# Larger rest bursts, paired score banks and a new order inside an attention slot

## The chip, the cores and the metric

The kernel runs on one core of a Trainium2 chip. TensorE (PE) multiplies, PEld is its weight load, VectorE (DVE) and ScalarE (ACT) read the product banks (PSUM, eight banks of 512 fp32 values in each of 128 partitions), GpSimd (POOL) and SyncE (SP) start DMAs. The metric is the device time of one execution in microseconds; less is better.

## The reference, cut to what matters

```python
xn = layernorm(A_x)                                   # 2048 tokens x 576
q  = (xn @ wq) -> 32 heads of 128                     # wq is 576 x 4096
k, v = last 512 rows of the caches, 16 heads, each used by 2 query heads
p  = softmax(q k^T / sqrt(128));  o = p v
s  = o.reshape(2048, 4096) @ wo                       # wo is 4096 x 576
g  = silu(B(xn))                                      # layernorm, gelu, shifts, w1, w2, w3, w4
out = A_x + s * g
```

The 576 input columns are four full chunks of 128 rows and a rest of 64 rows. The change concerns the attention, `s`.

## The kernel before, in words

The 2048 tokens are four blocks of 512. One attention "slot" `u` (0 to 127) is one query head of one block, `u = block * 32 + head`. In a slot the kernel issues the four score products of head `u` (`stage_s`, a 128x512 bank each: 128 keys by 512 tokens), the query product of head `u+1` (`stage_q`), and the value products of head `u-1` (`stage_v`, two halves of eight 128x129 matmuls; the 129th column of `v_sb` is one, so that it gives the softmax's denominator). ACT takes the exponential of each score bank into `pT`. DVE copies the finished query product to `qT` (bf16), inverts the denominators and scales the value products into `o`. SP transposes `o` by DMA into `oT`, and in the slots from `WO0 = 45` and from 65 and 97 PE also multiplies an earlier block's `oT` by `wo`, in five groups, one in a slot: four of 32 matmuls with 512 columns (L269, copied out by ACT at L279) and a fifth, of 128 matmuls with 64 columns, for the last 64 output columns (copied out at L291). The product of the last block stands around the last slots and behind them.

The query product of a head is four matmuls with 128 rows of `wq` (L526) and one with the 64 rest rows. The first four heads (`PLAIN`) take the rest as a fifth matmul padded with zeros. For all others the rest is computed for four heads together (`rest_q`, L511): two matmuls with 64 rows each stand side by side on the two halves of PE's rows, for two of the heads straight into their query banks, for the other two into two score banks. ACT copies those two to `rq` (L516, 128x512 each), and DVE adds `rq` while it makes `qT` (L534). The rest weights are loaded with every block of `wq` (`load_wq`, L339 and L346), 30 times in all, on POOL's queue.

PSUM holds three single score banks (`ps_sc`), two query banks (`ps_pq`), two value banks (`ps_po`) and one bank for the `wo` product (`ps_wo`). The finished `o` of 18 heads fit in `o_pool`.

The order of PE, SP and POOL is written out by hand (`manual_schedule`) in a loop over the slots; ACT's and DVE's order is set by a planner when the program is built. Small steps of layernorm for later blocks are put into slots by `fill`, transposes by `turn`, the `wo` products by `pe_fill`. The beginning, before slot 0, is written out for all engines: transposes of the first block on PE into three score banks (L470), copies to `xT_b` on DVE (L478) and ACT (L476), key transposes (L486), and the first two heads' query products (L707).

The stretch behind the attention (the MLP branch B and the end) starts some 466 us into the span. The change touches none of its lines.

Of the kernel before, what the change touches and what calls it, by code (L numbers as in the profile page):

```python
# [8 lines left out]
P = 128  # L9
ACT = mybir.ActivationFunctionType  # L10
ALU = mybir.AluOpType
# [20 lines left out]
def kernel(  # L32
# [266 lines left out]
    with ExitStack() as actx:  # L299
# [10 lines left out]
        wq_b = [res.tile([P, NDC, 4 * Dh], BF16, name=f"wq_b{i}") for i in range(NWQ)]  # L310
# [37 lines left out]

# [16 lines left out]
        def prep_k(g):  # L365
            st = {}
            src = kst_t[g // 4][:, (g % 4) * W:(g % 4 + 1) * W]

            def tr(kc):
                if kc == 0:  # L370
                    st["ps"] = ps_wo.tile([P, W], BF16, name="ps_k", tag="wo")
                nc.tensor.transpose(out=st["ps"][:, kc * P:(kc + 1) * P], in_=src[:, kc * P:(kc + 1) * P],
                                    identity=ident[:, :])
                if kc == KCH - 1:
                    with tc.high_priority(offset=HP):
                        nc.vector.tensor_copy(out=kT[:, g, :], in_=st["ps"][:, :])

            return [lambda kc=kc: tr(kc) for kc in range(KCH)]

# [15 lines left out]
        for w in wq_b:  # L395
            nc.gpsimd.memset(w[DR:, NF, :], 0.0)
        with tc.manual_schedule(engines={SP}):
            load_k(0, nc.sync, 2)
            for m0 in (0, 2 * Dh):
                cols = slice(m0, m0 + 2 * Dh)  # L400
                nc.sync.dma_start(out=wq_b[0][:, 0:NF, cols],
# [998 lines left out]
```

## Time and profile before

| what | us |
|---|---|
| median of three runs | 817.04 (816.65 to 817.09) |
| the profiled execution's own time | 817.54 |
| its span, first to last instruction | 815.9 |
| PE busy | 804.7 |
| ACT busy | 445.4 |
| DVE busy | 445.6 |

The span is what the profile's times are counted in; the execution's own time lies 1.6 us above it. Matmuls overlap, so a matmul's own duration (379 ns for 512 columns) is longer than the distance to the next one in an undisturbed row of them; distances are read from the timeline, where several equal instructions stand as one row with their count, the start of the first and the time to the end of the last.

### The profile page before, as it was taken

Reading aid. Unit: us, or ns where it says so; the run is one execution under the profiler, and the core shown is the slowest. Engines: PE = TensorE matmul, PEld = TensorE weight load, DVE = VectorE, ACT = ScalarE, POOL = GpSimd, SP = SyncE. Lnnn points to the kernel's source line nnn. Section 1 sums busy time; section 2 is a strip of 40 time slices with the busy share of each in tenths; the row PEclk is TensorE's granted clock in tenths of the full one; section 3 lists DMA queues with packets and bytes.
Section 4 is the critical chain, followed back from the end, with each engine's and each line's share of the span. In section 5 each row is a group of like instructions: output and inputs, shape, how many; then the busy total and the mean of one; then the engine's idle time right before and its main releaser. Section 6 shows DMA issues by size and latency. Waiting matters only on the chain. (4 is left out here: it accounts for less than half of the span.)

```text
span 815.9 us, 19891 instructions
## 1 busy us (share of the span) xinstructions
PE 804.7 (99%) x8157; PEld 469.0 (57%) x8239; DVE 445.6 (55%) x1379; ACT 445.4 (55%) x798; POOL 125.2 (15%) x211
## 2 busy tenths in 40 slices
PE   9999999999999999999999999999999999999997
PEld 6655655466545666545666556555555555555555
DVE  6868685128832679642566439353246636655413
ACT  7888887338833788833888542033343333335620
POOL 3333321201101111100210301272000000000000
PEclk9999999999999999999999999999999999999999
DMA  7995998109842756410674461399100410330101
GB/s 210 170 186 153 169 190 144 59 9 165 167 70 59 147 97 136 109 45 14 132 133 81 83 93 59 92 303 229 55 2 16 93 44 16 48 89 16 45 15 39
DMA packets 137710, 81.26 MB, mean 100 GB/s; under 512 B 114288, under 2 KB 127888, under 8 KB 137616
## 3 DMA queue, kind: packets, MB, share of 16 engines
q1 hardware_dynamic: 123536, 39.85, 29.2%
q0 software_dynamic: 12832, 38.85, 18.8%
q8 instruction: 65, 1.06, 0.6%
q10 hardware_dynamic: 1248, 1.25, 0.4%
q14 instruction: 29, 0.24, 0.1%
HBM read 46.89 MB, written 6.93 MB: 66 GB/s over the span
## 5 line engine op out<-in xcount | busy, mean ns | idle before, releaser
L549 ACT ACTIVATE pT<-sc 128x512 bf16<-128x512 f32 x512 | 286.7, 599 | 95.7 <-PE sc L545 80.0
L545 PE MATMUL sc<-qT,kT 128*128 128x512 bf16 x507 | 168.5, 379 | 0.1
L564 PEld LDWEIGHTS <-pT 128*128 128x128 bf16 x2048 | 134.5, 98 | 52.6 <-issue 11.0
L564 PE MATMUL po<-v_sb,pT 128*128 128x129 bf16 x2048 | 158.0, 220 | 0.3
L1033 PE MATMUL ph<-xT_b,w_s 64*128 64x512 bf16 x976 | 127.4, 376 | 0.0
L526 PE MATMUL psq<-xT_b,wq_b 128*128 128x512 bf16 x451 | 121.8, 379 | 3.0
L1070 PE MATMUL pm<-w_s,h 64*128 64x512 bf16 x864 | 122.2, 377 | 0.0
L1051 ACT ACTIVATE h<-ph 128x512 bf16<-128x512 f32 x67 | 39.4, 597 | 132.7 <-PE ph L1033 130.5
L569 DVE TENSOR_TENSOR o<-po,ri_b 128x256 bf16<-128x256 f32 x256 | 107.8, 421 | 6.4
L1070 PEld LDWEIGHTS <-h 64*128 64x128 bf16 x1728 | 71.1, 94 | 54.9
L269 PE MATMUL pswo<-wo_sb,oT 128*128 128x512 bf16 x434 | 101.3, 379 | 0.6
L269 PEld LDWEIGHTS <-oT 128*128 128x128 bf16 x1024 | 64.8, 98 | 54.3
L1070 PE MATMUL pr<-w_s,h 64*128 64x64 bf16 x864 | 90.3, 189 | 0.0
L536 DVE CAST qT<-psq 128x512 bf16<-128x512 f32 x64 | 44.0, 688 | 74.2 <-PE psq L511 42.9
L1033 PEld LDWEIGHTS <-w_s 64*128 64x128 bf16 x1152 | 56.1, 94 | 48.2 <-issue 0.6
L526 PEld LDWEIGHTS <-wq_b 128*128 128x128 bf16 x506 | 49.4, 98 | 59.3 <-issue 0.8
L534 DVE TENSOR_TENSOR qT<-psq,rq 128x512 bf16<-128x512 f32 x62 | 42.8, 691 | 69.7 <-ACT pT L549 59.7
L1049 DVE COPY hx<-ph 128x512 f32<-128x512 f32 x55 | 38.0, 692 | 60.3 <-PE ph L1033 60.3
L339 POOL DMA_DIRECT2D wq_b<-in_A_wq_dram x30 | 23.1, 770 | 264.6 <-PE sc L545 252.7
L568 DVE RECIPROCAL ri_b<-po 128x2 f32<-128x2 f32 x256 | 42.4, 165 | 32.0 <-PE po L564 26.7
L545 PEld LDWEIGHTS <-kT 128*128 128x128 bf16 x512 | 45.7, 98 | 20.7 <-DVE qT L534 0.5
L516 ACT ACTIVATE rq<-sc 128x512 f32<-128x512 f32 x62 | 33.6, 594 | 8.2 <-PE sc L511 8.2
(168 smaller groups left out, 700.2 us busy)
## 6 DMA issues: line engine op xcount, KB each, us to landing
wq_b<-in_A_wq_dram POOLq DMA_DIRECT2D x30, 512.0 KB, 4.7
wo_sb<-in_A_wo_dram POOLq DMA_DIRECT2D x8, 576.0 KB, 7.0
w_s<-in_B_w_dram POOLq DMA_DIRECT2D x9, 512.0 KB, 6.0
w_s<-in_B_w_dram POOLq DMA_DIRECT2D x10, 288.0 KB, 5.0
w_s<-in_B_w_dram POOLq DMA_DIRECT2D x4, 576.0 KB, 5.6
s_b<-s_dram SPq DMA_DIRECT2D x4, 576.0 KB, 7.3
x_b<-in_A_x_dram SPq DMA_DIRECT2D x4, 576.0 KB, 7.6
out_dram<-o SPq DMA_DIRECT2D x15, 144.0 KB, 1.8
```

The source lines that it names most:

```text
L269: nc.tensor.matmul(ps, lhsT=oT_t[qb * Hq + h][:, tt, :], rhs=wo_sb[:, h, lo:hi], start=(i == 0), stop=(i == Hq - 1))
L526: nc.tensor.matmul(psq[:, :], lhsT=w[:, kc, hh * Dh:(hh + 1) * Dh], rhs=xT_b[qb % 2][:, kc, :], start=(kc == 0 and not (two and hh == 1)), ...
L534: behind["qT"] = nc.vector.tensor_tensor(out=qT[:, :], in0=psq[:, :], in1=rq_t.pop(u)[:, :], op=ALU.add)
L536: nc.vector.tensor_copy(out=qT[:, :], in_=psq[:, :])
L545: nc.tensor.matmul(sc[:, :], lhsT=kT[:, g, kc * P:(kc + 1) * P], rhs=qT_t[u][:, :], start=True, stop=True)
L549: behind["exp"] = nc.scalar.activation(out=pT[:, :], in_=sc[:, :], func=ACT.Exp, scale=SCALE)
L564: nc.tensor.matmul(po[:, j, :], lhsT=pTs[kc][:, tt * P:(tt + 1) * P], rhs=v_sb[:, g, kc, 0:Dh + 1], start=(kc == 0), stop=(kc == KCH - 1))
L568: nc.vector.reciprocal(out=ri, in_=po[:, :, Dh])
L569: nc.vector.tensor_tensor(out=o[:, t0:t0 + 2, :], in0=po[:, :, 0:Dh], in1=ri.unsqueeze(2).to_broadcast([P, 2, Dh]), op=ALU.mult)
L1033: nc.tensor.matmul(ps[i][:, :], lhsT=lhsT, rhs=xT[half, kc, :], start=first, stop=last, skip_group_check=True)
L1051: nc.scalar.activation(out=h3[:, :], in_=src[:, :], func=ACT.Gelu_apprx_tanh)
L1070: nc.tensor.matmul(out, lhsT=h3_t[b, fc][half, tt * P:(tt + 1) * P], rhs=w4_s[fc // WS][half, fc % WS, lo:hi], start=key not in started, s ...
```

## The change

- The rest is computed for six heads at a time (16 times) or for four (7 times), by a list of first heads, `BURSTS`. The first two of a burst go into their query banks as before; the next two into the second score pair, the last two of six into the first pair. ACT copies the first of these pairs with one 128x1024 instruction (L528); of the other, DVE copies one half (L525) and ACT the other (L526).
- The rest weights of all heads stay in `wr_sb` (128 x 16 x 128), loaded once by `load_wr`. The plain heads' rest weights lie in `wr_first`, a part of `wo_sb` that is filled later.
- The score banks are two pairs (`sc0`, `sc1`) of two banks each. `stage_s(u, i)` writes a pair with two matmuls, and one 128x1024 exponential reads it (L560).
- The bank for the `wo` product is gone: in the slots with a `wo` group the group's bank is the first half of `sc1`, and both halves of the scores go through `sc0`.
- The order in a slot is: query product, scores of pair 0, fill, values, scores of pair 1, values, with the `wo` matmuls in four parts between. In a slot that issues a burst (`late_q`) the scores of pair 0 come first, and both halves of the values stand ahead of pair 1; if such a slot has a `wo` group too (49, 69 and 101: the fifth groups), that group's first part follows the first scores at once.
- At the beginning the transposes go into one tile of two banks (four chunks) and the other tile (the fifth chunk and two key heads).
- `o_pool` has 12 tiles, and five more lie in `xn_b[3]` until that block is loaded: 17 in place of 18.
- `prep_k` had no caller left and goes.

```diff
--- before.py
+++ after.py
...
         PLAIN = 4
-        wq_b = [res.tile([P, NDC, 4 * Dh], BF16, name=f"wq_b{i}") for i in range(NWQ)]
+        BURSTS = [(4, 6), (10, 6), (16, 6), (22, 6), (28, 4), (32, 6), (38, 6), (44, 6), (50, 4), (54, 4), (58, 6),
+                  (64, 6), (70, 4), (74, 6), (80, 6), (86, 6), (92, 4), (96, 6), (102, 4), (106, 6), (112, 6), (118, 6),
+                  (124, 4)]
+        SPARE = 5
+        spare = xn_b[NB - 1][:].rearrange("p t d -> p (t d)")
+        WO0 = Hq + 13
+        wo_slots = {b * Hq + 1 + i if b > 1 else WO0 + i for b in range(1, NB) for i in range(TB + 1)}
+        x_at = (9, Hq + 14, 2 * Hq + 4)
+        wq_b = [res.tile([P, NF, 4 * Dh], BF16, name=f"wq_b{i}") for i in range(NWQ)]
+        wr_sb = res.tile([P, Hq // 2, Dh], BF16, name="wr_sb")
+        wr_first = wo_sb[:, PLAIN, 0:PLAIN * Dh]
         ri_b = res.tile([P, Hq, TB], FP32, name="ri_b")
...
         qT_pool = pool("qT_pool", 3)
-        pT_pool = pool("pT_pool", 4)
-        pT2_pool = pool("pT2_pool", 3)
-        o_pool = pool("o_pool", 18)
-        ps_sc = pool("ps_sc", 3, PSUM)
+        pT_pool = pool("pT_pool", 5)
+        o_pool = pool("o_pool", 12)
+        ps_sc = pool("ps_sc", 1, PSUM)
         ps_pq = pool("ps_pq", 2, PSUM)
         ps_po = pool("ps_po", 2, PSUM)
-        ps_wo = pool("ps_wo", 1, PSUM)
...
-            eng.dma_start(out=w[:, 0:NF, :],
-                              in_=A_wq[0:NF * P, c0:c0 + 4 * Dh].rearrange("(kc p) m -> p kc m", p=P))
-            if j < PLAIN // 4:
-                eng.dma_start(out=w[0:DR, NF, :], in_=A_wq[NF * P:D, c0:c0 + 4 * Dh])
-                return
-            last = A_wq[NF * P:D, c0:c0 + 4 * Dh].rearrange("p (j two m) -> p j two m", two=2, m=Dh)
+            eng.dma_start(out=w[:, :, :],
+                          in_=A_wq[0:NF * P, c0:c0 + 4 * Dh].rearrange("(kc p) m -> p kc m", p=P))
+            if 1 < j < 8:
+                load_wr(j + 1, 1, eng)
+        def load_wr(j, n, eng):
+            j = j % 8
+            last = A_wq[NF * P:D, :].rearrange("p (j two m) -> p j two m", two=2, m=Dh)
             for k in range(2):
-                eng.dma_start(out=w[k * DR:(k + 1) * DR, NF, 0:2 * Dh].rearrange("p (j m) -> p j m", j=2),
-                              in_=last[:, :, k, :])
+                eng.dma_start(out=wr_sb[k * DR:(k + 1) * DR, 2 * j:2 * (j + n), :],
+                              in_=last[:, 2 * j:2 * (j + n), k, :])
...
             load_wq(1, nc.sync)
+            load_wr(1, 2, nc.sync)
...
         def x_banks():
-            pairs = [ps_sc.tile([P, 2, QB], BF16, name="ps_x", tag="sc") for _ in range(3)]
-            return [pairs[kc // 2][:, kc % 2, :] for kc in range(NDC)]
+            four = [ps_sc.tile([P, 4, QB], BF16, name="ps_x", tag=f"sc{i}") for i in range(2)]
+            return [four[kc // 4][:, kc % 4, :] for kc in range(NDC)], four[1][:, 2:4, :]
...
-        def keys_first(g0, psp, tag):
-            ps = psp.tile([P, 2, W], BF16, name="ps_k2", tag=tag)
+        def keys_first(g0, ps):
...
+        bursts, first_of = {}, {}
+        for u0, n in BURSTS:
+            bursts[u0] = n
+            for i in range(n):
+                first_of[u0 + i] = u0
+        def score_bank(i):
+            return ps_sc.tile([P, 2, QB], FP32, name="sc", tag=f"sc{i}")
+        def wq_main(u, kc):
+            cols = slice(u % 4 * Dh, (u % 4 + 1) * Dh)
+            return wq_b[(u // 4) % NWQ][:, kc, cols] if kc < NF else wr_first[:, cols]
         def rest_q(u, first):
-            w, xT = wq_b[(u // 4) % NWQ], xT_b[u // Hq % 2]
+            xT = xT_b[u // Hq % 2]
             psq_t[u + 1] = ps_pq.tile([P, QB], FP32, name="psq", tag="pq")
-            pss = [first, psq_t[u + 1]] + [ps_sc.tile([P, QB], FP32, name="sc", tag="sc") for _ in range(2)]
+            n = bursts[u]
+            pair = [score_bank(i) for i in ((0,) if u - 1 in wo_slots else (1, 0)[0:n // 2 - 1])]
+            pss = [first, psq_t[u + 1]] + [p[:, i, :] for p in pair for i in range(2)]
             for i, ps in enumerate(pss):
                 half = slice(i % 2 * DR, (i % 2 + 1) * DR)
-                nc.tensor.matmul(ps[:, :], lhsT=w[half, NF, i // 2 * Dh:(i // 2 + 1) * Dh], rhs=xT[half, NF, :],
+                nc.tensor.matmul(ps[:, :], lhsT=wr_sb[half, (u + i) % Hq // 2, :], rhs=xT[half, NF, :],
                                  start=(i > 0), stop=(i != 1), skip_group_check=True)
-            for i in (2, 3):
-                rq_t[u + i] = rq_pool.tile([P, QB], FP32, name="rq")
+            for k, p in enumerate(pair):
+                rq = rq_pool.tile([P, 2, QB], FP32, name="rq")
                 with tc.high_priority(offset=HP):
-                    behind["rq"] = nc.scalar.activation(out=rq_t[u + i][:, :], in_=pss[i][:, :], func=ACT.Copy)
+                    if k:
+                        nc.vector.tensor_copy(out=rq[:, 0, :], in_=p[:, 0, :])
+                        nc.scalar.activation(out=rq[:, 1, :], in_=p[:, 1, :], func=ACT.Copy)
+                    else:
+                        nc.scalar.activation(out=rq[:], in_=p[:], func=ACT.Copy)
+                for i in range(2):
+                    rq_t[u + 2 + 2 * k + i] = rq[:, i, :]
         def stage_q(u):
-            qb, h = divmod(u, Hq)
-            w = wq_b[(u // 4) % NWQ]
-            hh = h % 4
-            two = u >= PLAIN
-            psq = psq_t.pop(u) if two and hh == 1 else ps_pq.tile([P, QB], FP32, name="psq", tag="pq")
-            n = NF if two else NDC
+            qb = u // Hq
+            plain = u < PLAIN
+            pos = 0 if plain else u - first_of[u]
+            psq = psq_t.pop(u) if pos == 1 else ps_pq.tile([P, QB], FP32, name="psq", tag="pq")
+            n = NDC if plain else NF
             for kc in range(n):
-                nc.tensor.matmul(psq[:, :], lhsT=w[:, kc, hh * Dh:(hh + 1) * Dh], rhs=xT_b[qb % 2][:, kc, :],
-                                 start=(kc == 0 and not (two and hh == 1)), stop=(kc == n - 1 and not (two and hh == 0)),
+                nc.tensor.matmul(psq[:, :], lhsT=wq_main(u, kc), rhs=xT_b[qb % 2][:, kc, :],
+                                 start=(kc == 0 and pos != 1), stop=(kc == n - 1 and (plain or pos != 0)),
                                  skip_group_check=True)
-            if two and hh == 0:
+            if not plain and pos == 0:
                 rest_q(u, psq)
...
             with tc.high_priority(offset=HP):
-                if two and hh >= 2:
-                    behind["qT"] = nc.vector.tensor_tensor(out=qT[:, :], in0=psq[:, :], in1=rq_t.pop(u)[:, :], op=ALU.add)
+                if pos >= 2:
+                    behind["qT"] = nc.vector.tensor_tensor(out=qT[:, :], in0=psq[:, :], in1=rq_t.pop(u), op=ALU.add)
                 else:
...
-        def stage_s(u, kc):
+        def stage_s(u, i):
             g = (u % Hq) // REP
-            if kc == 0:
-                pT_t[u] = []
-            first = u == 0 and kc == KCH - 1
-            sc = (ps_po if first else ps_sc).tile([P, QB], FP32, name="sc", tag="po" if first else "sc")
-            nc.tensor.matmul(sc[:, :], lhsT=kT[:, g, kc * P:(kc + 1) * P], rhs=qT_t[u][:, :], start=True, stop=True)
-            if kc == 1:
-                pair_t[u] = pT2_pool.tile([P, 2, QB], BF16, name="pT2")
-            pT = pair_t[u][:, kc - 1, :] if kc in (1, 2) else pT_pool.tile([P, QB], BF16, name="pT")
-            behind["exp"] = nc.scalar.activation(out=pT[:, :], in_=sc[:, :], func=ACT.Exp, scale=SCALE)
-            pT_t[u].append(pT)
-            if kc == KCH - 1:
+            sc = score_bank(0 if u in wo_slots else i)
+            for j in range(2):
+                kc = 2 * i + j
+                nc.tensor.matmul(sc[:, j, :], lhsT=kT[:, g, kc * P:(kc + 1) * P], rhs=qT_t[u][:, :], start=True,
+                                 stop=True)
+            pT = pT_pool.tile([P, 2, QB], BF16, name="pT")
+            nc.scalar.activation(out=pT[:], in_=sc[:], func=ACT.Exp, scale=SCALE)
+            pT_t.setdefault(u, []).extend(pT[:, j, :] for j in range(2))
+            if i == 1:
                 qT_t.pop(u)
...
             if t0 == 0:
-                o_t[u] = o_pool.tile([P, TB, Dh], BF16, name="o")
+                i = u % (12 + SPARE)
+                if i < SPARE and u < x_at[2] - 2 * SPARE:
+                    o_t[u] = spare[:, i * QB:(i + 1) * QB].rearrange("p (a b) -> p a b", a=TB)
+                else:
+                    o_t[u] = o_pool.tile([P, TB, Dh], BF16, name="o")
             o = o_t[u]
...
             oT = oT_pool.tile([P, TB, P], BF16, name="oT")
-            nc.sync.dma_start(out=oT[:], in_=o[:].rearrange("p a b -> p (a b)"), transpose=True)
+            nc.sync.dma_start(out=oT[:], in_=o[:, :, :].rearrange("p a b -> p (a b)"), transpose=True)
             oT_t[u] = oT
...
             def bank(shape, name):
-                return ps_pq.tile(shape, FP32, name=name, tag="pq") if last else ps_wo.tile(shape, FP32, name=name, tag="wo")
+                if last:
+                    return ps_pq.tile(shape, FP32, name=name, tag="pq")
+                half = score_bank(1)[:, 0, :]
+                return half if len(shape) == 2 else half[:, 0:TB * R0].rearrange("p (t r) -> p t r", t=TB)
...
-            pss = x_banks()
+            pss, k01 = x_banks()
             tr1_first(pss, range(1))
-            k01 = keys_first(0, ps_wo, "wo")
+            keys_first(0, k01)
             tr1_first(pss, range(1, TB))
             xT_first(pss)
-            k23 = keys_first(2, ps_po, "po")
+            k23 = keys_first(2, ps_po.tile([P, 2, W], BF16, name="ps_k2", tag="po"))
             nc.vector.tensor_copy(out=kT[:, 0:2, :], in_=k01[:, :, :])
...
             for u in range(0, max(max(fill), max(pe_fill)) + 1):
-                atoms = pe_fill.get(u, []) + [fn for v, g in pe_late if v == u for fn in prep_k(g)]
+                atoms = pe_fill.get(u, [])
                 n = len(atoms)
-                c0, c1, c2 = (n // 2, n // 2, 3 * n // 4) if u == U else (2 * (u == U - 1), n // 3, 2 * n // 3)
-                cut = [atoms[c0:c1], atoms[c1:c2], atoms[c2:]]
+                cuts = [0, n // 4, n // 2, 3 * n // 4, n]
+                if u == U:
+                    cuts = [0, n // 2, n // 2, 3 * n // 4, n]
+                def wo_part(i):
+                    for fn in atoms[cuts[i]:cuts[i + 1]]:
+                        fn()
+                def scores(i):
+                    if u < U:
+                        stage_s(u, i)
+                def values(t0):
+                    if 0 <= u - 1 < U:
+                        stage_v(u - 1, t0)
                 if u == 1:
                     stage_q(2)
-                for i in range(4):
-                    if u < U and not (i == 1 and trip(u)):
-                        stage_s(u, i)
-                    if i == 0:
-                        if trip(u):
-                            stage_s(u, 1)
-                        if 1 < u < U - 1:
-                            stage_q(u + 1)
-                        for fn in fill.get(u, []) + atoms[0:c0]:
-                            fn()
-                        continue
-                    if i < 3 and 0 <= u - 1 < U:
-                        stage_v(u - 1, 2 * (i - 1))
-                    for fn in cut[i - 1]:
-                        fn()
+                late_q = u + 1 in bursts
+                if late_q:
+                    scores(0)
+                    if u in wo_slots:
+                        wo_part(0)
+                if 1 < u < U - 1:
+                    stage_q(u + 1)
+                if not late_q:
+                    scores(0)
+                for fn in fill.get(u, []):
+                    fn()
+                if not (late_q and u in wo_slots):
+                    wo_part(0)
+                values(0)
+                wo_part(1)
+                if late_q:
+                    values(2)
+                    wo_part(2)
+                    scores(1)
+                else:
+                    scores(1)
+                    wo_part(2)
+                    values(2)
+                wo_part(3)
                 for fn in turn.get(u, []):
...
```

More of the change, by code (lines that the diff above doesn't have):

```diff
@@ L394 @@
         nc.gpsimd.memset(xn_b[0][:, :, D:], 0.0)
-        for w in wq_b:
-            nc.gpsimd.memset(w[DR:, NF, :], 0.0)
+        nc.gpsimd.memset(wr_first[DR:, :], 0.0)
         with tc.manual_schedule(engines={SP}):
@@ L682 @@
             mv, nb = ln1_first()
-            wu = ps_sc.tile([P, QB], FP32, name="warm", tag="sc")
+            wu = ps_sc.tile([P, QB], FP32, name="warm", tag="sc0")
             def warm(n):
@@ L706 @@
                 for kc in kcs:
-                    nc.tensor.matmul(psq[u][:, :], lhsT=wq_b[0][:, kc, u * Dh:(u + 1) * Dh], rhs=xT_b[0][:, kc, :],
+                    nc.tensor.matmul(psq[u][:, :], lhsT=wq_main(u, kc), rhs=xT_b[0][:, kc, :],
                                      start=(kc == 0), stop=(kc == NDC - 1))
```

23 lines of the change are left out of this document (2 added, 21 removed).

## The prediction

> **What bounds the kernel now.** I read the page's span and busy line first, then the windows by stage, PE's waits, and the timeline of one slot with a burst.
>
> ```profile
> span 815.9 us, 19891 instructions
> PE 804.7 (99%) x8157; PEld 469.0 (57%) x8239; DVE 445.6 (55%) x1379; ACT 445.4 (55%) x798; POOL 125.2 (15%) x211
> 20.00:140.00 120.00, 118.79 (x1048) 72.53 (x1067) 89.23 (x292) 104.26 (x190) 37.26 (x62) 1.00 1.02 173
> 226.00:270.00 44.00, 43.69 (x364) 23.96 (x369) 11.62 (x37) 14.55 (x26) 4.34 (x8) 1.00 0.29 57
> ```
>
> PE is busy throughout, at full granted clock (the 1.00 behind the engines), while ACT, the next engine, is busy 104 of 120 us in the densest stretch. The DMA share there is 1.02: DMAs are saturated from 20 to 140 us.
>
> ```profile
> PEld L511 <- issue: 13.1, 31, 0.4
> PEld L564 <- issue: 11.0, 26, 0.4
> PEld L526 <- DMA wq_b<-in_A_wq_dram: 0.6, 1, 0.6
> PEld L545 <- DVE qT L534: 0.5, 2, 0.2
> PEld L545 <- DVE qT L536: 0.2, 1, 0.2
> ```
>
> PE's weight loads wait for other engines in four places only; what is left is the 31 rest bursts (L511) and the return from them (L564). One burst, from the timeline (start, time to the last end, engine, line, tiles, count), with one row of the groups (busy us, mean ns, idle) ahead of it:
>
> ```profile
> L564 PE MATMUL po<-v_sb,pT 128*128 128x129 bf16 x2048 | 158.0, 220 | 0.3
> 120.03 0.59 PE L526 MATMUL psq<-xT_b,wq_b 128*128 128x512 bf16 x2
> 120.55 0.39 PE L511 MATMUL psq<-xT_b,wq_b 64*128 64x512 bf16 x2
> 120.78 0.38 PE L511 MATMUL sc<-xT_b,wq_b 64*128 64x512 bf16 x2
> 121.09 0.63 PE L564 MATMUL po<-v_sb,pT 128*128 128x129 bf16 x8
> 121.19 1.09 ACT L516 ACTIVATE rq<-sc 128x512 f32<-128x512 f32 x2 [0.26 <-PE sc L511]
> ...
> 122.66 1.03 PE L526 MATMUL psq<-xT_b,wq_b 128*128 128x512 bf16 x4
> 123.52 0.38 PE L545 MATMUL sc<-qT,kT 128*128 128x512 bf16 x1
> 123.73 0.62 PE L564 MATMUL po<-v_sb,pT 128*128 128x129 bf16 x8
> 123.94 2.42 ACT L549 ACTIVATE pT<-sc 128x512 bf16<-128x512 f32 x4 [0.19 <-PE sc L545]
> ```
>
> Distances: a 512-column matmul starts (1.03 - 0.38) / 3 = 0.216 us before the next, a 129-column one (0.62 - 0.22) / 7 = 0.057. So a slot is 8 x 0.216 + 16 x 0.057 = 2.64 us. The last L526 starts at 120.03 + 0.59 - 0.38 = 120.24; to the first rest pair it is 0.31, to the second 0.23, and 0.31 from there to the values. A change into 64-row matmuls and back thus costs 2 x 0.095 = 0.19 us. ACT starts 0.42 after the start of the matmul it waits for (123.52 to 123.94), 0.41 after a rest matmul. PE has no other idle time in the attention, so only the changes of mode and those few waits can be won.
>
> **The change part by part.** *Fewer bursts.* PE's instruction count is unchanged; 23 bursts instead of 31, with the same 62 pairs, save 8 x (0.31 + 0.31 - 0.22 - 0.22) = **-1.45 us**, fully on PE.
>
> *Order in a slot.* The query product comes first and its `qT` is used a slot later behind the next query product, so the three waits for `qT` go: each delayed PE by under 0.1 us: **-0.2**. The wait for `wq_b` (0.3 us of PE) may stay: the weights are read 0.43 us earlier in that slot, but from the ninth load of `wq` on (j = 8) POOL issues no rest loads beside it. (Until then it issues the same two with each, and SP's queue at the beginning holds two rest loads in the place of two.) Zero, bounds -0.3 and +0.4.
>
> *Double exponential.* No 1024-element ACT instruction from PSUM is in the trace. The prices:
>
> ```profile
> L549 ACT ACTIVATE pT<-sc 128x512 bf16<-128x512 f32 x512 | 286.7, 599 | 95.7 <-PE sc L545 80.0 <-PE po L564 3.9
> L516 ACT ACTIVATE rq<-sc 128x512 f32<-128x512 f32 x62 | 33.6, 594 | 8.2 <-PE sc L511 8.2
> L279 ACT ACTIVATE so<-pswo 128x512 bf16<-128x512 f32 x14 | 8.4, 597 | 33.6 <-PE pswo L269 33.6
> L291 ACT ACTIVATE so<-pswr 128x256 bf16<-128x256 f32 x3 | 1.1, 383 | 2.4 <-PE pswr L269 2.4
> L536 DVE CAST qT<-psq 128x512 bf16<-128x512 f32 x64 | 44.0, 688 | 74.2 <-PE psq L511 42.9 <-PE psq L526 31.4
> L219 DVE BATCH_NORM_STATS2 ln_st<-xn_b 128x6 f32<-128x288 bf16 x32 | 13.7, 436 | 0.0
> L220 DVE BATCH_NORM_AGGREGATE ln_mv<-ln_st 128x2 f32<-128x12 f32 x16 | 3.2, 201 | 0.0
> L109 DVE SCALAR_TENSOR_TENSOR nr_t<-nr_y 128x4 f32<-128x4 f32 x21 | 3.4, 160 | 0.3
> 205.72 0.68 DVE L534 TENSOR_TENSOR qT<-psq,rq 128x512 bf16<-128x512 f32 x1
> 206.45 0.11 PEld L545 LDWEIGHTS <-kT 128*128 128x128 bf16 x2 [0.22 <-DVE qT L534]
> ```
>
> 256 more elements cost 597 - 383 = 214 ns, so 1024 take 599 + 428 = **1.03 us**; bounds 0.60 (the second bank free) and 1.20 (twice L549). I take 1.03, since the slope is of the same source. Two L516 take 1.09, so the next may start 0.10 before an instruction's end. PE follows an evacuation by 0.05 us (206.40 to 206.45). *The Trainium skill, "ScalarE: Activation LUTs" (What ACT_TABLE_LOAD costs), gives 186 ns + 0.833 ns per element without pointer operands, an estimate of 1.04 us; it gives 0.61 for 512, where the trace has 0.599. By it the waits below would add 0.3 us.*
>
> Plain slot (0 at its first matmul): query 0 to 0.86, pair 0 to 1.30, values to 1.75, pair 1 to 2.19, values to 2.64. First exponential 1.08 + 0.42 = 1.50 to 2.53, second 2.43 to 3.46, which is 0.82 in the next slot. The values there need it at 1.41: nothing waits.
>
> Slot that issues a burst: pair 0 at 0 needs the exponential that ended 2.53 (slack 0.06). Its own runs 0.72 to 1.75. Query 0.43 to 1.30, rest pairs at 1.39, 1.62 and, into pair 0, at 1.85 (slack 0.05). ACT's 1024 copy of the second rest pair runs 1.62 + 0.41 = 2.03 to 3.05, so `sc1` is free at 3.10. Both value halves now stand ahead of pair 1, which PE reaches at 1.85 + 0.31 + 0.91 = 3.07 with six heads, at 2.84 with four. It waits 0.03 in the 16 bursts of six (**+0.5**) and 0.26 in the four bursts of four that use `sc1` (28, 54, 92, 124): **+1.05**.
>
> *The third rest pair.* In the built order ACT's half (L526) waits for DVE's copy (L525), and the second exponential of that head stands behind both. DVE: `qT` 1.82 to 2.51, half to 3.20, ACT's half 3.23 to 3.82, exponential 3.74 to 4.77. The value matmul that needs it comes at 3.53 + 1.30 + 0.11 = 4.94: slack of 0.12. In six of the 16 bursts (10, 22, 38, 58, 64, 86) the planner put layernorm steps before the copy, one aggregate (0.20) and a small step (as L109, 0.16) behind the cast and statistics (0.44 each) ahead of it: 0.35 to 0.4 late, so PE waits some 0.25 each, **+1.5** (bounds 0 and 4.5, the latter if nothing overlaps on DVE).
>
> *The `wo` bank.* It is now half of `sc1`, and one bank as before, but in slots 49, 69 and 101, burst slots with the fifth group, that group's first matmuls follow the first scores at once. The bank is still read by L279: its last matmul starts 0.22 before the slot, so 0.20 + 0.60 + 0.05 = 0.85, while PE comes at 0.43. **+1.25** for three (behind the slot's query product, as in before, it was hidden).
>
> *The beginning.*
>
> ```profile
> 8.07 1.00 PE L470 MATMUL ps_x<-ident,xn_b 128*128 128x128 bf16 x15
> L478 DVE COPY xT_b<-ps_x 128x512 bf16<-128x512 bf16 x3 | 1.1, 418 | 1.0 <-PE ps_x L470 1.0
> 8.95 1.09 DVE L478 COPY xT_b<-ps_x 128x512 bf16<-128x512 bf16 x3 [0.97 <-PE ps_x L470]
> 9.06 1.08 ACT L476 ACTIVATE xT_b<-ps_x 128x512 bf16<-128x512 bf16 x2 [0.85 <-PE ps_x L470]
> 9.42 2.32 PE L707 MATMUL psq<-xT_b,wq_b 128*128 128x512 bf16 x9
> 10.92 0.69 DVE L711 CAST qT<-psq 128x512 bf16<-128x512 f32 x1 [0.29 <-PE psq L707]
> 11.66 1.02 PE L545 MATMUL sc<-qT,kT 128*128 128x512 bf16 x4
> ```
>
> Four chunks share one tile. In the built order DVE's first copy waits for the fourth chunk's transpose (two of 0.056 later: 9.06), and ACT's two wait for DVE's second (9.06 + 0.34 + 0.42 = 9.81): 9.85 to 10.44 and 10.34 to 10.93. So chunk 2 is multiplied at 10.49, chunk 3 at 10.98, chunk 4 at 11.20, the cast comes at 11.62 instead of 10.92: **+0.70**, and all of PE's stream shifts. In slot 1 the values wait for the second exponential, which ends some 2.4 us behind the first pair: **+0.2**.
>
> *At nothing.* ACT's fewer instructions, DVE's 16 copies (11 us) and POOL's fewer rest loads lie beside PE. If the saturated DMAs deliver the 17 `o` buffers later than 18 were needed, the cover is gone; that is a rival. SP's order of transposes is the same. Behind 466 us nothing changes; bounds -0.3 and +0.3.
>
> Sum: -1.45 - 0.2 + 0.5 + 1.05 + 1.5 + 1.25 + 0.9 = **+3.55**. The profiled execution's 817.54 becomes 821.1; it lies 0.5 above the median, so in medians 817.04 + 3.55 = **820.6 us**.
>
> **The rivals.**
> 1. *Not slower: the double instruction is cheap.* With 0.85 us in place of 1.03, sixes and layernorm slots wait for almost nothing (0.4 together), the fours 0.09 each, slot 1 not at all: 0.4 + 0.35 + 1.25 + 0.7 - 1.65 = +1.05, **818.1**. Below some 0.90 (+1.6) the change is within the limit of what can be told, 0.2% or 1.6 us. For it: no 1024 row. Against: 383 to 597 ns for 256 more elements.
> 2. *Faster: PE does not wait for whole reads of a bank pair*, in the bursts, the fifth groups and at the beginning alike: -1.65, **815.4**; it decides as soon as less than 1.6 of the 5.2 us of waits come. Against it: PE followed DVE's end by 0.05 us above, and the waits are in the built order.
> 3. *Slower still: DMAs.* With the share at 1.02, `o` buffers and `wq` come late around 95 to 110 us, or DVE's steps do not overlap at all: +1.5 to +3 more, **822.8**. For it: the 0.6 us wait on `wq_b`. Against: slower slots give DMAs time.
>
> **How the numbers follow.** Forecast 0.60, rival 1 0.17, rival 2 0.08, rival 3 0.15. The range from 816.8 to 822.8 leaves out rival 2, half of rival 3 and little else. Slower by over 0.2% (above 818.7): most of the forecast and rival 3, 0.70; within 0.2%: rival 1 and the forecast's edge, 0.21; faster: rival 2 and a rest, 0.09. The forecast alone: 819.0 to 822.3.
>
> **What would show it.** 23 groups of L519 with 0.31 on both sides; L560's mean near 1.03 us; a gap in PE of 0.4 us at the fifth `wo` groups, of 0.26 ahead of pair 1 in slots 27, 53, 91 and 123; the first scores at 12.36 instead of 11.66; weight loads of L579 waiting for ACT in the slots behind bursts 10, 22 and 38. The prediction is wrong if L560 takes under 0.9 us, or if PE's waits lie in other places.

## The result, and the profile after

The changed kernel takes 820.34 us (median of six runs, 820.11 to 820.44), the kernel before 816.74 us (six runs, 816.38 to 817.09). The ratio is 1.0043 with a 95% interval of 1.003 to 1.0056: the change makes the kernel 3.6 us slower, as forecast (820.6). A second set of five runs of the changed kernel gave 820.72 us and a ratio of 1.0046 (1.0032 to 1.0059).

The page of the changed kernel (span and busy time), and its groups of instructions:

```profile
span 818.9 us, 19757 instructions
PE 805.9 (98%) x8158; PEld 471.3 (58%) x8239; DVE 458.5 (56%) x1395; ACT 412.2 (50%) x519; POOL 95.4 (12%) x162
...
L560 ACT ACTIVATE pT<-sc 128x1024 bf16<-128x1024 f32 x256 | 250.2, 1022 | 114.8 <-PE sc L557 106.6 <-PE sc L269 7.0 <-ACT pT L560 0.3
L528 ACT ACTIVATE rq<-sc 128x1024 f32<-128x1024 f32 x23 | 23.6, 1024 | 10.3 <-PE sc L519 10.3
L525 DVE COPY rq<-sc 128x512 f32<-128x512 f32 x16 | 10.9, 681 | 0.0
L526 ACT ACTIVATE rq<-sc 128x512 f32<-128x512 f32 x16 | 9.6, 597 | 4.3 <-DVE rq L525 3.5
```

ACT is busy 412 us instead of 445, POOL 95 instead of 125, and the kernel is slower all the same: neither was the bound. The double exponential (L560) takes 1.022 us. PE's waits after:

```profile
PEld L519 <- issue: 9.7, 23, 0.4
PEld L579 <- issue: 6.4, 22, 0.4
PEld L269 <- issue: 1.6, 3, 0.5
PEld L579 <- ACT pT L560: 1.6, 6, 0.4
PEld L557 <- issue: 1.3, 6, 0.2
PE sc L269 <- ACT so L279: 0.8, 3, 0.3
```

The 31 bursts are 23 (the first row; the second is the return from them, of which it counts 22). In exchange there are waits that the kernel before did not have: three of the fifth `wo` groups (L269, the third and the last row), six of the value products for an exponential (L579 on ACT), and those of the scores (L557).

Where the time lies, by milestones of PE in the traces (us from the start of the span; the first matmul behind the attention is that of the branch B, L823, before L790):

| | before | before, again | after | after, again |
|---|---|---|---|---|
| first key transpose starts | 7.51 | 7.35 | 7.36 | 7.51 |
| first scores | 11.66 | 11.42 | 12.15 | 12.30 |
| first matmul behind the attention | 475.87 | 475.33 | 479.06 | 479.21 |
| span | 815.9 | 815.1 | 818.9 | 820.0 |
| first key transpose to first scores | 4.15 | 4.07 | 4.79 | 4.79 |
| first scores to the end of the attention | 464.21 | 463.92 | 466.90 | 466.92 |

So 0.64 to 0.72 us arise in the beginning and 2.7 to 3.0 us between the first scores and the end of the attention. Behind it nothing is changed; that stretch takes 339.3 to 340.8 us in the fourteen profiles here, without order.

Three timelines of the changed kernel show the waits. First slot 27, which issues a burst of four heads and copies its rest pair out of `sc1` (columns: start, time to the last end, engine, line, operation, tiles, form, count):

```profile
87.42 0.39 PE L519 MATMUL psq<-xT_b,wr_sb 64*128 64x512 bf16 x2
87.64 0.38 PE L519 MATMUL sc<-xT_b,wr_sb 64*128 64x512 bf16 x2
87.95 1.08 PE L579 MATMUL po<-v_sb,pT 128*128 128x129 bf16 x16
88.06 1.02 ACT L528 ACTIVATE rq<-sc 128x1024 f32<-128x1024 f32 x1 [0.26 <-PE sc L519]
89.14 0.59 PE L557 MATMUL sc<-qT,kT 128*128 128x512 bf16 x2
```

The last value matmul starts at 87.95 + 1.08 - 0.22 = 88.81, and the scores could follow at 88.87. ACT's copy ends at 89.08, and they start at 89.14: 0.27 us. Next slot 9, with a burst of six beside layernorm steps:

```profile
37.49 0.67 DVE L549 CAST qT<-psq 128x512 bf16<-128x512 f32 x1
37.72 1.08 PE L579 MATMUL po<-v_sb,pT 128*128 128x129 bf16 x16
38.08 0.20 DVE L220 BATCH_NORM_AGGREGATE ln_mv<-ln_st 128x2 f32<-128x12 f32 x1
38.31 0.17 DVE L103 TENSOR_SCALAR nr_v<-ln_mv 128x4 f32<-128x4 f32 x1
38.39 0.68 DVE L525 COPY rq<-sc 128x512 f32<-128x512 f32 x1
38.68 0.59 PE L557 MATMUL sc<-qT,kT 128*128 128x512 bf16 x2
39.11 0.60 ACT L526 ACTIVATE rq<-sc 128x512 f32<-128x512 f32 x1 [0.48 <-DVE rq L525]
39.60 2.09 ACT L560 ACTIVATE pT<-sc 128x1024 bf16<-128x1024 f32 x2
40.41 0.78 PE L579 MATMUL po<-v_sb,pT 128*128 128x129 bf16 x8
40.67 0.34 PEld L579 LDWEIGHTS <-pT 128*128 128x128 bf16 x6 [0.17 <-ACT pT L560]
```

Two layernorm steps stand between the cast and DVE's half of the third rest pair; ACT's half waits 0.48 us for it, the exponential stands behind that, and the eight value matmuls take 0.78 instead of 0.62 us. Last slot 49:

```profile
175.39 0.59 PE L557 MATMUL sc<-qT,kT 128*128 128x512 bf16 x2
175.59 0.60 ACT L279 ACTIVATE so<-sc 128x512 bf16<-128x512 f32 x1 [2.82 <-PE sc L269]
176.24 1.09 PE L269 MATMUL sc<-wo_sb,oT 128*128 128x64 bf16 x32 [0.25 <-ACT so L279]
```

The second score matmul starts at 175.60; the fifth `wo` group could start at 175.82 and starts at 176.24, when L279 has left the bank.

### The profile page after: what moved, and what is told of

The parts are those of the page before. It is cut to its first block, busy times and chain, and to the rows that moved or that the text cites. A ratio compares the mean times of both kernels' runs of the same rounds, so it can differ in the third digit from the quotient of the medians.

```text
span 818.9 us, 19757 instructions
## 1 busy us (share of the span) xinstructions
PE 805.9 (98%) x8158; PEld 471.3 (58%) x8239; DVE 458.5 (56%) x1395; ACT 412.2 (50%) x519; POOL 95.4 (12%) x162
## 3 DMA queue, kind: packets, MB, share of 16 engines
q10 hardware_dynamic: 1248, 1.25, 0.5%
## 4 chain that ended last, share of the span: by engine, by line
PE 93%; DVE 4%; ACT 1%; issue 1%; POOL 0%; DVEq 0%; ACTq 0%; POOLq 0%
PE ph L1066 14%; PE po L579 13%; PE sc L557 12%; PE psq L539 12%; PE sc L269 12%; PE pm L1103 11%; PE pm L1281 4%; PE pm L1066 3%; PE pm L823 2%; PE pswo L269 2%; PE pr L1103 2%; PE ph L823 1%; PE pr L269 1%; PE sc L519 1%; PE pm L269 1%
## 5 line engine op out<-in xcount | busy, mean ns | idle before, releaser
L560 ACT ACTIVATE pT<-sc 128x1024 bf16<-128x1024 f32 x256 | 250.2, 1022 | 114.8 <-PE sc L557 106.6
L579 PEld LDWEIGHTS <-pT 128*128 128x128 bf16 x2048 | 133.4, 98 | 57.9 <-issue 6.4
L579 PE MATMUL po<-v_sb,pT 128*128 128x129 bf16 x2048 | 156.0, 220 | 0.7 <-ACT pT L560 0.4
L557 PE MATMUL sc<-qT,kT 128*128 128x512 bf16 x507 | 151.0, 379 | 0.4
L269 PE MATMUL sc<-wo_sb,oT 128*128 128x512 bf16 (+1 forms) x756 | 101.8, 284 | 1.6 <-ACT so L279 0.8
L269 PEld LDWEIGHTS <-oT 128*128 128x128 bf16 x1024 | 65.2, 98 | 56.3 <-issue 1.6
L584 DVE TENSOR_TENSOR o<-po,ri_b 128x256 bf16<-128x256 f32 x216 | 91.2, 422 | 6.3 <-DVE ri_b L583 0.3
L547 DVE TENSOR_TENSOR qT<-psq,rq 128x512 bf16<-128x512 f32 x78 | 53.9, 691 | 32.3 <-PE psq L539 31.7
L539 PEld LDWEIGHTS <-wq_b 128*128 128x128 bf16 x504 | 45.9, 98 | 41.6
L557 PEld LDWEIGHTS <-kT 128*128 128x128 bf16 x512 | 45.2, 98 | 29.7 <-issue 1.3
L549 DVE CAST qT<-psq 128x512 bf16<-128x512 f32 x48 | 33.0, 688 | 41.6 <-PE psq L519 25.9
L1084 ACT ACTIVATE h<-hx 128x512 bf16<-128x512 f32 x55 | 34.6, 630 | 6.0 <-DVE hx L1082 1.7
```

The costliest lines, as they stand in the source:

```text
L269: nc.tensor.matmul(ps, lhsT=oT_t[qb * Hq + h][:, tt, :], rhs=wo_sb[:, h, lo:hi], start=(i == 0), stop=(i == Hq - 1))
L539: nc.tensor.matmul(psq[:, :], lhsT=wq_main(u, kc), rhs=xT_b[qb % 2][:, kc, :], start=(kc == 0 and pos != 1), stop=(kc == n - 1 and (plain ...
L547: behind["qT"] = nc.vector.tensor_tensor(out=qT[:, :], in0=psq[:, :], in1=rq_t.pop(u), op=ALU.add)
L557: nc.tensor.matmul(sc[:, j, :], lhsT=kT[:, g, kc * P:(kc + 1) * P], rhs=qT_t[u][:, :], start=True, stop=True)
L560: nc.scalar.activation(out=pT[:], in_=sc[:], func=ACT.Exp, scale=SCALE)
L579: nc.tensor.matmul(po[:, j, :], lhsT=pTs[kc][:, tt * P:(tt + 1) * P], rhs=v_sb[:, g, kc, 0:Dh + 1], start=(kc == 0), stop=(kc == KCH - 1))
```

## The experiments

Each kernel is the changed one with the edit shown. The ratio is to the kernel before, run beside it on the same chip (medians of 816.82 to 816.92 us). Since single waits are about as large as the spread of the runs (most lie within 2 us of each other), I read the trace beside the time: from the first key transpose to the first scores ("beginning", 4.79 us after the change), and from the first scores to the end of the attention ("attention", 466.9).

| kernel | median us (runs) | ratio to before, 95% interval | beginning | attention |
|---|---|---|---|---|
| the change, again | 820.72 (5) | 1.0046, 1.0032 to 1.0059 | 4.79 | 466.92 |
| transpose banks by engine | 820.62 (5) | 1.0049, 1.0035 to 1.0063 | 4.30 | 467.00 |
| the same, again | 820.36 (5) | 1.0044, 1.003 to 1.0058 | 4.31 | 467.03 |
| exchanged banks behind bursts of four | 820.21 (5) | 1.0039, 1.0025 to 1.0052 | 4.80 | 465.98 |
| fifth `wo` group behind the query product | 819.38 (7) | 1.003, 1.0019 to 1.0041 | 4.80 | 465.67 |
| third rest pair on DVE | 818.83 (8) | 1.0026, 1.0016 to 1.0037 | 4.82 | 465.24 |
| all four | 816.76 (12) | 0.9995, 0.998 to 1.001 | 4.30 | 463.53 |
| all four, bursts of four only | 818.18 (12) | 1.0014, 1.0005 to 1.0022 | 4.29 | 465.32 |
| single exponentials | 822.69 (4) | 1.0073, 1.0054 to 1.0092 | 4.82 | 468.72 |
| scores first in every slot | 827.79 (4) | 1.0129, 1.011 to 1.0149 | 4.79 | 473.60 |
| all four, bursts of four, scores first | 842.11 (4) | 1.0307, 1.0292 to 1.0323 | 4.84 | 488.77 |

**Transpose banks by engine.**

```diff
-            return [four[kc // 4][:, kc % 4, :] for kc in range(NDC)], four[1][:, 2:4, :]
+            return [four[j][:, i, :] for j, i in ((0, 0), (0, 1), (1, 0), (1, 1), (1, 2))], four[0][:, 2:4, :]
```

> The changed kernel, but at the beginning each of the two transpose banks is read by one engine alone (DVE's two chunks in one, ACT's two and the last in the other). Theory A (the waits of the sum cost what they last, each by itself): DVE's first copy no longer waits for the fourth chunk and ACT's copies no longer wait for DVE's second, so the first scores come at about 11.5 us instead of 12.15 and the time falls by 0.5 to 0.7 us, to 819.7. Theory B (what is won early is lost to the next wait, above all to the wq_b load that lands at about 9.6 us, so that waits do not add up): the first scores move by under 0.25 us and the time stays within 0.2 us of 820.3.

Run again beside the kernel before and the changed one, on one chip:

> The kernel before once more, beside the next two on one chip: how far its first scores and its time move from one execution to the next. Theory A (what varies is when the first keys and weights land): first scores between 11.6 and 12.6 us, the rest of the trace the same to 0.1 us. Rival: it is as steady as the first profile, 11.66, and the later beginnings seen in the experiments are the change's.

> The changed kernel once more, on the same chip: 820.3 us; first scores between 12.1 and 13.1 us, from the first scores to the first matmul behind the attention 466.9 us as in the first profile.

> The changed kernel with transpose banks by engine, on the same chip as the changed kernel itself. Theory A (the wait of the two engines on each other costs what it lasts): 0.5 us faster than the changed kernel, first scores 0.5 us earlier for the same landing of the first keys. Theory B (the first query weights, landing at 9.3 to 9.9 us, take its place): the same time within 0.2 us.

The beginning of the changed kernel, and then that of the edited one:

```profile
7.36 0.62 PE L479 MATMUL ps_x<-ident,stage 128*128 128x128 bf16 x8
8.80 1.09 DVE L472 COPY xT_b<-ps_x 128x512 bf16<-128x512 bf16 x3 [0.83 <-PE ps_x L464]
9.64 1.08 ACT L470 ACTIVATE xT_b<-ps_x 128x512 bf16<-128x512 bf16 x2 [1.45 <-DVE xT_b L472]
12.15 0.59 PE L557 MATMUL sc<-qT,kT 128*128 128x512 bf16 x2
```

```profile
7.32 0.61 PE L479 MATMUL ps_x<-ident,stage 128*128 128x128 bf16 x8
8.67 0.76 DVE L472 COPY xT_b<-ps_x 128x512 bf16<-128x512 bf16 x2 [0.66 <-PE ps_x L464]
8.84 1.09 ACT L470 ACTIVATE xT_b<-ps_x 128x512 bf16<-128x512 bf16 x2 [0.60 <-PE ps_x L464]
11.62 1.02 PE L557 MATMUL sc<-qT,kT 128*128 128x512 bf16 x4
```

ACT's copies start 0.80 us earlier, and the first scores follow the first key transpose by 4.30 instead of 4.79 us: the mechanism is shown, and the weights' landing does not take its place. In time it is not resolved: 0.36 us faster beside the changed kernel, with overlapping ranges. One new wait of 0.28 us (at 340 us, in both profiles of it, behind an exponential that starts 0.28 us later than in the changed kernel) makes the attention 0.1 us longer; why that exponential starts later stays open. The second profile of the kernel before has the first scores at 11.42, earlier than I expected, 4.07 us behind the first key transpose. That transpose starts between 7.3 and 8.4 us in the profiles of the changed kernels, with the landing of the first keys; the two profiles of the kernel before (7.51 and 7.35) do not show whether its beginning spreads as far.

**Exchanged banks behind bursts of four** (`fours`: the slots ahead of a burst of four, without `wo` slots).

```diff
+        fours = {u0 - 1 for u0, n in BURSTS if n == 4 and u0 - 1 not in wo_slots}
...
-            sc = score_bank(0 if u in wo_slots else i)
+            sc = score_bank(0 if u in wo_slots or u in fours else 1 - i if u - 1 in fours else i)
```

> The changed kernel, but in the four bursts of four heads that use the second double bank for their rest pair, the second pair of scores goes into the first bank (its exponential is long done), and the next slot uses the two banks in exchanged order. Theory A: the four waits of 0.27 us in slots 27, 53, 91 and 123 go, nothing else moves, the last scores come 1.07 us earlier (463.6 instead of 464.65), the time is 819.3. Theory B (PE runs into the next exponential instead, because ACT is the one that is late in these slots): waits of 0.2 us or more appear ahead of the scores or values of the slot after, and less than half of the 1.07 us is won.

Slot 27 in that kernel:

```profile
88.85 1.08 PE L581 MATMUL po<-v_sb,pT 128*128 128x129 bf16 x16
89.77 0.59 PE L559 MATMUL sc<-qT,kT 128*128 128x512 bf16 x2
```

The scores follow the last value matmul (88.85 + 1.08 - 0.22 = 89.71) without a wait, and so in all four slots; in the second slot after each of them (29, 55, 93, 125) 0.05 us of a new wait stands ahead of the scores, so that the attention is 0.93 us shorter. Theory A for the trace; the median (0.13 us) does not show it, and in the profile the first keys landed at 8.20 us, where they landed at 7.31 in the changed kernel's.

**Fifth `wo` group behind the query product.**

```diff
-        def stage_q(u):
+        def stage_q(u, ahead=lambda: None):
...
             if not plain and pos == 0:
+                ahead()
                 rest_q(u, psq)
...
                 if late_q:
                     scores(0)
-                    if u in wo_slots:
-                        wo_part(0)
                 if 1 < u < U - 1:
-                    stage_q(u + 1)
+                    stage_q(u + 1, lambda: wo_part(0) if u in wo_slots else None)
```

> The changed kernel, but in slots 49, 69 and 101 the first quarter of the fifth wo group stands behind the main query product instead of right behind the first scores. Theory A: the three waits of 0.42 us go (PE reaches the bank at 1.30 us of the slot, it is free at 0.85), the time falls by 1.25 us to 819.1. Theory B: the rest pair behind it, which uses the first score bank, or the values then wait for ACT, and less than half of the 1.25 us is won.

Slot 49 in that kernel:

```profile
176.41 0.59 PE L558 MATMUL sc<-qT,kT 128*128 128x512 bf16 x2
176.85 1.03 PE L539 MATMUL psq<-xT_b,wq_b 128*128 128x512 bf16 x4
177.71 1.07 PE L269 MATMUL sc<-wo_sb,oT 128*128 128x64 bf16 x31
```

The `wo` group follows the last query matmul (176.85 + 1.03 - 0.38 = 177.50) after the usual 0.21 us. The three waits are gone and nothing took their place: the attention is 1.24 us shorter, the time 0.96.

**Third rest pair on DVE.**

```diff
-                        nc.vector.tensor_copy(out=rq[:, 0, :], in_=p[:, 0, :])
-                        nc.scalar.activation(out=rq[:, 1, :], in_=p[:, 1, :], func=ACT.Copy)
+                        nc.vector.tensor_copy(out=rq[:], in_=p[:])
```

> The changed kernel, but DVE alone copies the third rest pair (1024 elements), so that no ACT copy and no exponential stands behind DVE's layernorm steps. Theory A: the waits of 0.16 to 0.38 us of the values behind bursts 10, 22, 38, 58, 64 and 86 go, 1.5 us in all, and DVE's longer copy is done before the bank is needed: 818.8. Theory B (DVE is now the late one: the longer copy, some 1.1 to 1.3 us, delays the first scores of the next slot or the values' results): new waits on DVE in several of the 16 bursts of six, time 820.3 or more.

Groups and the timeline of slot 9 in that kernel:

```profile
L525 DVE COPY rq<-sc 128x1024 f32<-128x1024 f32 x16 | 19.5, 1216 | 0.0
...
38.25 1.22 DVE L525 COPY rq<-sc 128x1024 f32<-128x1024 f32 x1
39.30 1.02 ACT L559 ACTIVATE pT<-sc 128x1024 bf16<-128x1024 f32 x1 [0.74 <-PE sc L556]
40.33 0.62 PE L578 MATMUL po<-v_sb,pT 128*128 128x129 bf16 x8
```

DVE's copy is longer, but the exponential no longer stands behind it, and the values take 0.62 us again. The attention is 1.67 us shorter, the time 1.51. (The Trainium skill, "VectorE: DVE Perf Modes", in its section on the TRN2 errata, gives 120 + 1024 cycles at 0.96 GHz for such a copy out of PSUM, an estimate of 1.19 us; the trace has 1.216.)

**All four, and all four with bursts of four heads only.**

```diff
-        BURSTS = [(4, 6), (10, 6), (16, 6), (22, 6), (28, 4), ...
+        BURSTS = [(u0, 4) for u0 in range(PLAIN, NB * Hq, 4)]    # second kernel only
```

> All four edits together: transpose banks by engine, exchanged score banks in the four bursts of four, the fifth wo groups behind the query product, the third rest pair copied by DVE alone. Theory A (the waits add): 820.3 - 0.6 - 1.07 - 1.25 - 1.5 = 815.9, just below the kernel before (816.7), because what is left of the change is the 1.45 us of the saved bursts, the 0.5 us of vanished qT and wq_b waits, and 0.7 us of waits in bursts of six. Theory B (what is won is lost to the next wait): 818 or more. Theory C (DVE's longer copy is late, the rest holds): 817.4 or more.

> The kernel with all four edits, but with bursts of four heads throughout (31 instead of 23). Theory A (a burst costs 0.19 us for the two changes between 128-row and 64-row matmuls): 8 x 0.19 = 1.45 us more for the bursts, less the 16 waits of 0.04 us that the bursts of six have: 0.8 us slower than with six heads. Rival (the bursts of six cost more than they save, by the third pair's copy, the wait and a slower exit): the same time or faster than with six heads.

All four together win 3.58 us in time and 3.38 in the attention (the three edits alone add up to 3.84; one exponential that took 0.25 us longer than the others, at 454 us, and a 0.1 us wait of the values at 205 us, behind DVE's longer copy, account for most of the rest). The waits add, as theory A has it, in the trace; the four medians alone add up to 2.3 us only. The number comes out 0.9 us above the 815.9 expected: the kernel is level with the one before, not ahead of it. Some 0.35 us of that lie outside the span: the time of this kernel is 1.94 us above its span (median of its runs), that of the kernel before beside it 1.59, so that in the span (814.85 against 815.2 us) it is the shorter one. In the kernel with only the third rest pair on DVE it is 1.82, in the other kernels 1.5 to 1.6; the reason stays open. With bursts of four it is 1.42 us slower (1.79 in the attention), more than the 0.8 expected: the eight bursts cost 8 x 0.19 = 1.5, the waits of 0.04 us go, but the exchanged banks now cost 0.05 us behind 28 bursts instead of four.

**Single exponentials.**

```diff
-            nc.scalar.activation(out=pT[:], in_=sc[:], func=ACT.Exp, scale=SCALE)
+            for j in range(2):
+                nc.scalar.activation(out=pT[:, j, :], in_=sc[:, j, :], func=ACT.Exp, scale=SCALE)
```

> The changed kernel, but each double exponential of 1024 elements is two of 512 (two times 0.60 us instead of 1.02 us). If the order of the slot lives on the cheaper double instruction: ACT needs 2.4 of 2.64 us in a plain slot and falls behind in every slot with a burst, where the second pair of scores waits some 0.2 to 0.3 us more; 23 bursts give 5 us or more, 825 or above. If ACT has room enough (rival): within 1 us of 820.3.

The changed kernel in slot 9, two double exponentials and the second and third rest pair:

```profile
35.41 1.93 ACT L560 ACTIVATE pT<-sc 128x1024 bf16<-128x1024 f32 x2
37.19 0.60 PE L519 MATMUL sc<-xT_b,wr_sb 64*128 64x512 bf16 x4
```

With single exponentials, their group and the same place:

```profile
L561 ACT ACTIVATE pT<-sc 128x512 bf16<-128x512 f32 x512 | 266.1, 603 | 105.0 <-PE sc L557 97.4 <-PE sc L269 7.0
...
35.71 2.07 ACT L561 ACTIVATE pT<-sc 128x512 bf16<-128x512 f32 x4
37.49 0.74 PE L519 MATMUL sc<-xT_b,wr_sb 64*128 64x512 bf16 x4
```

It is 2.35 us slower, neither 5 nor nothing. ACT is not late for the second pair of scores (0.06 us in bursts of six, instead of 0.04). The loss is at another place: four exponentials in a row take 2.07 us where two double ones take 1.93, and in the 16 bursts of six the third rest pair, which goes into the bank of the last of them, waits 0.12 to 0.13 us, 2.0 in all. The waits behind layernorm steps get 0.8 us shorter, and the attention is 1.81 us longer; some 0.3 us of that are not traced. The double instruction alone is worth some 2 us in this order.

**Scores first in every slot**, in the changed kernel, and in the one with all four edits and bursts of four.

```diff
-                if late_q:
-                    scores(0)
-                    if u in wo_slots:
-                        wo_part(0)
+                scores(0)
+                if late_q and u in wo_slots:
+                    wo_part(0)
                 if 1 < u < U - 1:
                     stage_q(u + 1)
-                if not late_q:
-                    scores(0)
```

> The changed kernel, but the first pair of scores stands ahead of the query product in every slot, not only in those with a burst. If the new order itself matters (theory A holds that only the qT waits, 0.2 us, hang on it): 0.2 to 0.5 us slower by new waits of the scores for qT. Rival (the new order brings the first exponential so late in a plain slot that the burst slot behind it has no slack): 0.5 us or more faster.

> The kernel with all four edits and bursts of four throughout, but with the first scores ahead of the query product in every slot. In the changed kernel that order cost 7 us: the trace shows the scores of the slot behind a burst of six waiting 0.24 to 0.84 us for the copy of the third rest pair to leave their bank. Theory A (that copy alone is the cause): with bursts of four there is no third pair, so the time is within 1 us of 818.2. Rival (the order itself costs, through the query product or ACT): 4 us or more above it.

Both theories for the first were wrong: 7.45 us slower. Its waits and the timeline at slots 9 and 10:

```profile
PE sc L557 <- ACT rq L526: 3.8, 6, 0.7
...
39.16 0.59 PE L557 MATMUL sc<-qT,kT 128*128 128x512 bf16 x2
39.77 0.60 ACT L526 ACTIVATE rq<-sc 128x512 f32<-128x512 f32 x1 [0.66 <-DVE rq L525]
40.41 0.59 PE L557 MATMUL sc<-qT,kT 128*128 128x512 bf16 x2 [0.66 <-ACT rq L526]
```

The first scores of the slot behind a burst of six need `sc0`, from which ACT still copies the third rest pair. In the changed kernel the query product (4 x 0.216 = 0.86 us) stands between; without it PE waits 0.24 to 0.84 us in 16 slots, 7.1 us (three new waits of 0.40 us behind `wo` groups and the 1.5 us of the values' waits, which go, nearly cancel). My test of this cause, the second kernel, is spoiled by its own edit: it has no third pair, but the exchanged banks put the first scores of a slot into the bank of the exponential just issued:

```profile
24.95 1.02 ACT L560 ACTIVATE pT<-sc 128x1024 bf16<-128x1024 f32 x1 [0.24 <-PE sc L557]
26.02 0.59 PE L557 MATMUL sc<-qT,kT 128*128 128x512 bf16 x2 [0.72 <-DVE xn_b L584]
```

The exponential ends at 25.97 and the scores start 0.05 later (the releaser named, DVE, had been done); 0.88 us in 28 slots, 24.7 us in all. With the query product first, the same exchange costs 0.05. So both kernels show the price of a bank without that cover; that bursts of four would be free of it in the plain order of banks was not tried.

## Why the prediction was right

The terms of the sum, and what the traces have (extra distance between the starts of PE's matmuls):

| step of the prediction | forecast | measured |
|---|---|---|
| fewer bursts | -1.45 | -1.41 (31 x 0.190 to 23 x 0.195) |
| waits for `qT` | -0.2 | -0.18 |
| pair 1 in bursts of six | +0.5 | +0.72 (16 of 0.044 to 0.054) |
| pair 1 in four bursts of four | +1.05 | +1.07 |
| third rest pair behind layernorm steps | +1.5 | +1.53 (six of 0.16 to 0.38), and 0.08 ahead of one pair of scores |
| fifth `wo` groups | +1.25 | +1.25 (three of 0.417) |
| beginning, first scores | +0.70 | +0.64 to +0.72 |
| slot 1 | +0.2 | +0.14 |

The measured terms make +3.9, the forecast was +3.55, the medians differ by 3.60. From the attention alone the terms give 0.2 more than the two second profiles differ by (3.00). Half of that lies in the bursts: taken whole, from the last query matmul to the first value matmul, a burst costs 0.202 us beyond its matmuls before and 0.207 on average after, which makes -1.50 instead of -1.41; the last 0.1 us is not traced. The mechanism came as forecast, wait by wait; that the medians differ by almost exactly the sum is partly luck, since the terms as measured make 0.2 to 0.35 us more and the second set of runs of the changed kernel lies 0.4 us above the first.

*The price of the double instruction* decided it: 1.022 us against 1.03 taken. Rival 1 (0.85 us) falls with that row. The Trainium skill's estimate of 1.04 us ("ScalarE: Activation LUTs", What ACT_TABLE_LOAD costs) agrees with it within 2%.

*Sizes that were off.* The waits of pair 1 in bursts of six are 0.044 instead of 0.03 each, since a slack worked out to 0.03 us from rows with two decimals carries that error 16 times. The return from a burst of six costs 0.316 instead of 0.308 us.

*The wait for `wq_b`* was put at zero. The first profile of the kernel before has 0.27 us of extra distance at 108 us, beside that wait, and its second profile none: the quoted row was one execution's, and so nothing that a change could win or lose. In the changed kernel the first query product waits 0.2 us for `wq_b`, but the interval to the first scores is the same 4.79 us where it does not.

*Rival 2* (PE does not wait for whole reads) falls with the timelines above and with the edits, each of which gave back its wait. *Rival 3* (DMAs) has nothing to show: no wait of the attention is on an `o` buffer, and DVE's steps overlap as assumed. The DMA share of 1.02 from 20 to 140 us was one execution's: it is 0.91 in the second profile of the kernel before, and 0.91 and 0.86 after the change.

*The other side of it* the prediction did not see: it treated the new order of a slot as worth 0.2 us of `qT` waits. The order carries the six-head bursts: without it the change would have been 11 us slower, not 3.6.

## What to carry to other kernels

When two banks are joined under one instruction, cost every reader of either half: the saving in instructions lay on engines with room, while each longer or newly shared hold of a bank came due on the bound engine, here 5.5 us of new waits against 1.6 us saved. Lay out one slot with starts and ends from the profile and look at slacks below 0.1 us first, above all where a copy of one engine waits behind that of another. Such waits can be taken back one at a time: by moving work that does not need the held bank (here a query product) in between, by exchanging the banks, or by giving a copy to one engine alone; here that brought the kernel level with the one before, and no further.

## What the runs showed that I had not expected

- The beginning moves by about 1 us between the profiles of the changed kernels (two profiles each of three kernels lie within 0.25 us): the first keys land between 6.65 and 8.34 us in the fourteen profiles, and where they land late everything behind them shifts, while from the first key transpose to the first scores a kernel keeps its time to 0.1 us. Single terms below 1 us are read from intervals of the trace, not from medians.
- The place of the query product in a slot, which cost nothing to choose, is worth 7 us with bursts of six and 24 us with the exchanged banks, since PE stands still for as long as the bank is held, up to 0.88 us a slot.
- ACT's exponential takes 1.022 us for 1024 elements and 0.599 to 0.603 for 512; DVE copies 1024 in 1.216 us and 512 in 0.681. For both the second half costs less than the first (0.42 and 0.54 us).
- Two engines that read different halves of one bank pair follow each other in the built order (L526 behind L525, ACT's L470 behind DVE's L472), although each half is a bank of its own. At the beginning a tile for each engine split them; for the third rest pair no run shows that, since there one engine took both halves.
